# Linear attention and mixture of depths: k and v loaded by halves of partitions, and a reordered end

## Chip, cores and metric

One core of a Trainium2 chip runs the kernel. The metric is the device time of one execution in microseconds (us). The core has five engines that run side by side: TensorE (PE; its weight loads are listed apart as PEld), VectorE (DVE), ScalarE (ACT), GpSimd (POOL) and SyncE (SP). SP and POOL issue DMAs here. The trace comes from one profiled execution, whose own time stands beside its span below.

## The reference

Two blocks follow each other. The first is linear attention over 8 batches of 8 heads, 576 tokens, 64 columns; the second picks 128 of the 576 tokens of each batch and sends them through two dense layers.

```python
q_s = softmax(q, axis=-1)                  # over the 64 columns
k_s = softmax(k, axis=2)                   # over the 576 tokens
kv  = einsum('bhsd,bhse->bhde', k_s, v)
x   = einsum('bhsd,bhde->bhse', q_s, kv)   # then (B, S, H*D) = (8, 576, 512)
scores = x @ w_gate
for b in range(B):
    top = indices of the 128 highest scores[b]
    ye  = relu(x[b, top] @ w1) @ w2        # 512 -> 1024 -> 512
    out[b, top] = x[b, top] + sigmoid(scores[b, top])[:, None] * ye
```

All other rows of out are x. Everything is float32.

## The kernel before

The work is cut into 16 units: a unit is four heads of one batch, so a batch is two units. A head's 576 tokens are 64 runs of 9 tokens. The code writes T = 9, R = 5, N2 = 4, D = 64, P = 128.

**Loads (L118 to L162).** Raw tiles hold k, v and q, three buffers of each (LD = 3). Units 0 and 1 are "flat": a head pair lies on 128 partitions, 9 tokens each, one DMA of 128 partitions with rows of 2304 bytes. From unit 2 on, k and v are "paired": a head lies on all 128 partitions, 5 rows of tokens on each. A run of 9 tokens is split over two neighbouring partitions, 5 tokens on the even one and 4 on the odd one, so that each of k and v takes two DMAs, one to every second partition with 1280-byte pieces and one to the others with 1024-byte pieces (L152). The fifth row of the odd partitions is cleared beforehand (`clear`, L172), and its ones column in v is set to zero there (`fifth`, L311). q of the units in `TWICE` is loaded in a form that VectorE can transpose (L139), 32 partitions at a time; of those in `SPREAD`, the same list here, half of the four DMAs go through POOL's queue. The other q's come in two DMAs, five rows and four rows (L146). From unit 8 on, a load on SP's queue waits until at most DEEP = 4 of these loads are under way (`behind`, L158).

**A unit's arithmetic.** ScalarE takes exp of k (`k_exp`, L289) and of q (`q_exp`, L302 and L298) and copies v beside a column of ones (`v_copy`, L307). `kv_mm` multiplies k by v: for a flat unit in 64x64 quarters of the array (L331), for a paired unit with all 128 partitions as the contraction and two 64-column halves of the array side by side, 5 rows for each of 4 heads (L336). The ones column gives the denominators of k; `kv_out` (L345 to L349) divides and adds a score column. q is transposed on TensorE (`q_t`, L377, L384) or VectorE (`q_blocks`), `x_mm` multiplies it by kv (L405, L409, L414), `x_sums` and `x_scale` (L431 to L442) divide, and `x_store` writes the rows to out from two halves of the partitions, 0 to 63 and 64 to 127 (L452).

**A batch's search.** When a batch's two units are done, `score` sums the scores (L461), `score_row` spreads them over all partitions (TensorE L479, ScalarE L485), `compare` counts how many scores lie before each (L493, five on VectorE), `hits` marks the 128 highest (L510), `find` turns the marks into row numbers (TensorE L520, VectorE L524 to L526), and `fetch` gathers the rows from out with an indirect DMA on POOL (L534). `turn` transposes them (TensorE L571, copy to xT L579).

**The dense layers** are cut into pieces that fill TensorE between the units' steps: eight of `mlp1` (L591, 128x128 products; the ReLU is on ScalarE at L594) and eight of `mlp2` (L601, one 128x512 product each). `finish` scales and adds (L614) and `put` scatters the rows to out with an indirect DMA on POOL (L606).

**Order.** It is written by hand (`manual_schedule`), and each engine's queue runs in that order. The main loop (L793 to L941) has one step s per unit, from LAG = 3 to NU + LAG - 1 = 18. Step s holds the products of unit s, k by v of unit s + 1, exp and copies of later units, one dense layer of batch (s - 3) // 2, and the DMA queue of the step: store of unit s, then loads of k, v and q of unit s + 3. Steps 16 to 18 have no unit left: in 16 the last batch's rows are found and gathered, 17 is its first dense layer, 18 its second. `pieces(n, to)` runs dense pieces at that point of the order. In step 15 three pieces of `mlp1` stand ahead of the last score row (L912), and in step 16 two pieces of `mlp2` ahead of the last search (L879).

```python
        here, follows = s < NU, s + 1 < NU
        ends = s // 2 if here and s % 2 == 1 else None
        chosen = (s - 2) // 2 if s % 2 == 0 and s <= NU else None
```

Of the kernel before, what the change touches and what calls it, by code (L numbers as in the profile page):

```python
# [17 lines left out]
def kernel(  # L18
# [23 lines left out]
    nc = tc.nc  # L42
# [58 lines left out]
    LD = 3  # L101
    FLAT = 0, 1
    TWICE = (9, 11, 13, 14, 15)
    SPREAD = TWICE
    RR = 4 * R
# [12 lines left out]
    def load(u, which, after=None, split=False, flat=False, odd=None):  # L118
        b, qd = units[u]
        for what in which:  # L120
            src = {"q": q, "k": k, "v": v}[what]
            first = src[place(b), 4 * qd].offset
            dmas = []
            if flat:
                t = view(raw[what][u % LD], False)
# [9 lines left out]
            elif what == "q" and u in TWICE:  # L135
                t = raw[what][u % LD].rearrange("p (a n) d -> p a (n d)", a=2)
                for g in range(0, 4, 1 if odd is None else 2):
                    g, queue = (g + 1, nc.gpsimd) if odd else (g, nc.sync)
                    dmas.append(queue.dma_start(out=t[32 * g:32 * g + 32, :, :ROW],  # L139
                                                in_=bass.AP(tensor=src.tensor,  # L140
                                                            offset=first + g // 2 * 2 * SD + g % 2 * D // 2,
                                                            ap=[[2 * T * D, 32], [SD, 2], [1, ROW]])))
            elif what == "q":
                t = view(raw[what][u % LD], False)
                for r0, r1 in ROWS:
                    dmas.append(nc.sync.dma_start(out=t[:, :, r0:r1].rearrange("p i r d -> p i (r d)"),  # L146
                                                  in_=bass.AP(tensor=src.tensor, offset=first + r0 * D,
                                                              ap=[[T * D, P], [2 * SD, 2], [1, (r1 - r0) * D]])))
            else:
                t = view(raw[what][u % LD], True)  # L150
                for n, rows in ((1, N2), (0, R)):
                    dmas.append(nc.sync.dma_start(out=t[n::2, :, :rows].rearrange("p h r d -> p h (r d)"),  # L152
                                                  in_=bass.AP(tensor=src.tensor, offset=first + n * R * D,
                                                              ap=[[T * D, 64], [SD, 4], [1, rows * D]])))
            if after is not None:
# [8 lines left out]
    way = []  # L164
    DEEP = 4
    ROWS = (0, R), (R, T)
# [4 lines left out]

    def clear(u):  # L172
        for what in "kv":
            nc.gpsimd.memset(view(raw[what][u % LD], True)[:, :, N2], 0.0)

# [40 lines left out]
    nc.vector.tensor_scalar(valid, second_half, -1.0, 1.0, op0=OP.mult, op1=OP.add)  # L216
    even_p = const.tile([P, 1], I32, name="even_p")
    nc.gpsimd.iota(even_p, pattern=[[0, 1]], base=1, channel_multiplier=1)
    nc.vector.tensor_single_scalar(even_p, even_p, 1, op=OP.bitwise_and)
    even = const.tile([P, 1], F32, name="even")  # L220
    nc.vector.tensor_copy(out=even, in_=even_p)
    beyond = const.tile([P, 1], F32, name="beyond")
# [27 lines left out]
    nc.gpsimd.iota(whole.rearrange("p (b r) -> p b r", b=B), pattern=[[S, B], [1, R]], base=0, channel_multiplier=T)  # L250
    clear(2)
    dma_k = load(1, "k", flat=True)
# [39 lines left out]
    def q_exp(u, c):  # L292
        if c == 0:
            st["qe", u] = at.tile([P, T, 2, D], F32, tag="qe", name="qe")
        if u in TWICE and u not in FLAT:
            half = raw["q"][u % LD].rearrange("p (a n) (h s) -> p a n h s", a=2, h=2)[:, c, :, 0]
            to = st["qe", u].rearrange("p r i d -> p (r i d)").rearrange("p (a n s) -> p a n s", a=2, n=2 * T)
            nc.scalar.activation(out=to[:, c], in_=half, func=AF.Exp)  # L298
            return
        r0, r1 = ROWS[c]  # L300
        qr = raw["q"][u % LD][:, :2 * T].rearrange("p (i r) d -> p r i d", i=2)
        nc.scalar.activation(out=st["qe", u][:, r0:r1], in_=qr[:, r0:r1], func=AF.Exp)  # L302

    def v_copy(u, engine=nc.scalar):
# [3 lines left out]
        else:  # L308
            engine.tensor_copy(out=out_v, in_=in_v)

    def fifth(u):  # L311
        nc.gpsimd.tensor_copy(out=view(v_ones[u % 2], True)[:, :, N2, D:], in_=even[:, None].to_broadcast([P, 4, 1]))

    def kv_mm(u, crossed=False):
# [16 lines left out]
        for a in range(0 if u in FLAT else 2):  # L333
            for r in range(R):
                for i in range(2):
                    nc.tensor.matmul(out=kv_ps[part(i), a, :D + 1], lhsT=ke[:, 2 * i + a, r], rhs=vo[:, 2 * i + a, r],  # L336
                                     start=(r == 0), stop=(r == N2))
        st["kv", u] = [(slice(0, P), kv_ps[:, :, :D + 1])]
# [54 lines left out]
    def x_mm(u, a, wide=False, tag="x"):  # L393
# [5 lines left out]
        for r in range(R):  # L399
            for i, c in QUARTERS:  # L400
                to = x[part(c), i, r * C:(r + 1) * C]
                if r == N2:
                    if a == 0:
                        rows = by_token[part(i), c, r] if u in TWICE and u not in FLAT else qT[part(i), c, r, 0]
                        last = nc.tensor.matmul(out=to, lhsT=rows, rhs=kw[part(i), c], start=True, stop=True)  # L405
                    continue
                if wide:
# [4 lines left out]
                    continue  # L412
                rows = by_token[part(i), a, R * c + r] if u in TWICE and u not in FLAT else qT[part(i), a, r, c]
                last = nc.tensor.matmul(out=to, lhsT=rows, rhs=kw[part(i), a], start=True, stop=True)  # L414
# [189 lines left out]
    def put(b, n, o):  # L604
# [3 lines left out]
            in_=o[:m], in_offset=None)  # L608

    def finish(b, n):  # L610
        m = slots[n][1]
# [46 lines left out]
    def general():  # L658
        nonlocal FLAT
        FLAT = tuple(range(NU))  # L660
        for n in range(2):
            nc.gpsimd.memset(v_ones[n][:, :, D:], 1.0)
        for b in range(B):
# [79 lines left out]
    x_out(0, 0)  # L743
    clear(3)
    load(3, "kv")
# [10 lines left out]
    x_mm(1, 1)  # L756
    fifth(2)
    x_out(0, 1)
# [11 lines left out]
    q_t(2, 0, wide=True, later=True)  # L770
    clear(4)
    load(4, "kv")
# [13 lines left out]
    k_exp(3)  # L786
    fifth(3)
    v_copy(3)
    LAG = 3
    AFTER = {4: 2}  # L790
    QUEUE = {"odd": "x+0 kv+3 q+3", "even": "x+0 kv+3 q+3", 5: "x+0 kv+3 q+3 x-5 x-4"}
    number = good = None
    for s in range(LAG, NU + LAG):  # L793

# [175 lines left out]
```

## Time and profile before

| what | value |
|---|---|
| median of 3 runs | 208.74 us (208.12 to 213.29) |
| the profiled execution | 209.41 us, span 207.6 us |
| TensorE clock granted | 0.986 |
| PE, PEld, DVE, ACT, POOL busy | 193.1, 146.1, 127.0, 92.1, 40.9 us |
| DMA | 49.43 MB, mean 238 GB/s |
| L591 and L601 (dense layers) on PE | 61.8 and 58.4 us |
| L414 (x) and L336 (k by v) on PE | 22.0 and 19.4 us |
| indirect DMA xr (L534), out (L606) on POOL | 8.5 and 7.2 us |

The page sums busy time over the span, draws the span in 40 slices and follows the chain of work that ended last back from the last instruction. A busy TensorE is not a TensorE at its peak, since matmuls are pipelined and their ends are modelled; a matmul of float32 leaves two records, so that 20 products show as 40. Times in the timeline count from the start of the span. Where an engine's idle time is given, the bracket names what ended it. DMA share is the mean busy share of the core's 16 DMA engines; it may go slightly over 1.

### The profile page before, as it was taken

The numbers are of one execution on the slowest core, as the hardware profiler recorded it, in microseconds if no ns is written. First come the engines' busy times: TensorE is split into PE (matmuls) and PEld (weight loads), VectorE is DVE, ScalarE is ACT, GpSimd is POOL, SyncE is SP. The second block draws the span as 40 slices with busy tenths as digits, with TensorE's granted clock in tenths as the row PEclk, the third lists the DMA queues.
The fourth block names the chain that finished last, engine by engine and source line by source line (L and its number), as shares of the span: only waits on it lengthen the run. The fifth ranks groups of instructions, "written<-read, shape, count | busy, mean of one in ns | idle before, by whom it ended". The sixth has DMA issues, their size and how long they took to land.

```text
span 207.6 us, 6693 instructions
## 1 busy us (share of the span) xinstructions
PE 193.1 (93%) x2801; PEld 146.1 (70%) x2801; DVE 127.0 (61%) x392; ACT 92.1 (44%) x136; POOL 40.9 (20%) x110
## 2 busy tenths in 40 slices
PE   7988899999999999999999999999999999999940
PEld 3576788885698749974897569864896479459510
DVE  5776935897278636957684948766696766432010
ACT  4475877673655814772347516452364012111100
POOL 7302100202020403140222132040402030224010
PEclk9999999999999999999999999999999999999995
DMA  6999999999699999899999899999970434031101
GB/s 219 396 294 344 376 363 371 372 374 351 152 295 285 289 356 381 215 296 261 251 285 280 255 230 262 308 269 233 338 210 18 95 114 114 1 102 54 58 17 41
DMA packets 36599, 49.43 MB, mean 238 GB/s; under 512 B 2513, under 2 KB 30673, under 8 KB 36562
## 3 DMA queue, kind: packets, MB, share of 16 engines
q1 hardware_dynamic: 34336, 41.57, 64.8%
q0 software_dynamic: 2080, 7.06, 11.5%
q8 instruction: 24, 0.39, 0.8%
q10 hardware_dynamic: 146, 0.30, 0.5%
q14 instruction: 13, 0.11, 0.1%
HBM read 37.39 MB, written 11.53 MB: 236 GB/s over the span
## 4 chain that ended last, share of the span: by engine, by line
PE 68%; DMA 21%; DVE 2%; issue 2%; ACT 2%; SPq 1%; POOL 1%; POOLq 0%; ACTq 0%
PE mm L591 22%; PE mm L601 21%; DMA k<-in_k_dram 11%; PE x L414 7%; PE kv L336 6%; DMA xr<-out_dram,idx 6%; DMA out_dram<-xs 4%; PE mm L204 3%; PE x L384 2%; PE mm L571 2%; PE kv L479 1%; PE kv L331 1%; PE x L405 1%; PE x L377 1%; DVE xs L439 1%
## 5 line engine op out<-in xcount | busy, mean ns | idle before, releaser
L591 PE MATMUL mm<-xT,w 128*128 128x128 f32 x512 | 61.8, 278 | 0.5 <-DVE xT L579 0.3
L591 PEld LDWEIGHTS mm<-xT,w 128*128 128x128 f32 x512 | 58.7, 192 | 2.3 <-ACT xT L579 1.0
L601 PE MATMUL mm<-w,hT 128*128 128x512 f32 x128 | 58.4, 599 | 0.0
L601 PEld LDWEIGHTS mm<-w,hT 128*128 128x128 f32 x128 | 23.0, 190 | 23.5 <-issue 23.0
L493 DVE SCALAR_TENSOR_TENSOR junk<-srow,s,not_before 128x576 bf16<-128x576 f32 x40 | 32.7, 818 | 5.2 <-ACT srow L485 4.1
L289 ACT ACTIVATE ke<-k 128x1280 f32<-128x1280 f32 (+1 forms) x16 | 20.2, 1260 | 9.8 <-DMA k<-in_k_dram 9.8
L414 PE MATMUL x<-kv_w,qT 64*64 64x66 f32 x960 | 22.0, 222 | 2.1 <-issue 1.4
L439 DVE TENSOR_TENSOR xs<-x,qrec 128x640 f32<-128x640 f32 (+1 forms) x31 | 23.5, 757 | 0.6 <-issue 0.3
L414 PEld LDWEIGHTS x<-kv_w,qT 64*64 64x64 f32 x960 | 18.7, 133 | 5.2 <-issue 4.3
L307 ACT COPY v_ones<-v 128x1280 f32<-128x1280 f32 x14 | 17.6, 1259 | 6.2 <-DMA v<-in_v_dram 6.2
L336 PEld LDWEIGHTS kv<-v_ones,ke 128*64 128x64 f32 x560 | 17.5, 137 | 3.4 <-issue 2.4
L336 PE MATMUL kv<-v_ones,ke 128*64 128x65 f32 x560 | 19.4, 224 | 0.2 <-ACT srow L485 0.2
L614 DVE SCALAR_TENSOR_TENSOR o<-mm,g,xr 128x512 f32<-128x512 f32 x7 | 5.3, 751 | 23.2 <-PE mm L601 23.2
L534 POOL DMA_INDIRECT xr<-out_dram,idx x8 | 8.5, 1061 | 54.6 <-DVE no L526 15.2
L579 ACT COPY xT<-mm 128x512 f32<-128x512 f32 x7 | 4.1, 585 | 31.5 <-PE mm L571 31.5
L606 POOL DMA_INDIRECT out_dram<-o,idx x7 | 7.2, 1026 | 50.5 <-DVE o L614 43.1
L594 ACT ACTIVATE hT<-mm 128x512 f32<-128x512 f32 x16 | 9.5, 596 | 16.5 <-PE mm L591 16.4
L302 ACT ACTIVATE qe<-q 128x640 f32<-128x640 f32 (+1 forms) x22 | 13.9, 677 | 3.5 <-DMA q<-in_q_dram 3.5
L391 ACT COPY qT<-x 128x640 f32<-128x640 f32 (+1 forms) x18 | 10.8, 648 | 9.0 <-PE x L384 8.2
L345 DVE RECIPROCAL krec<-kv 128x2 f32<-128x2 f32 x16 | 2.7, 170 | 18.8 <-PE kv L336 16.4
L431 DVE RECIPROCAL qrec<-x 128x10 f32<-128x10 f32 (+1 forms) x31 | 6.6, 213 | 9.4 <-PE x L405 7.6
L485 ACT ACTIVATE srow<-kv 128x576 f32<-128x576 f32 x7 | 4.5, 648 | 15.2 <-PE kv L479 15.2
(120 smaller groups left out, 187.3 us busy)
## 6 DMA issues: line engine op xcount, KB each, us to landing
out_dram<-xs SPq DMA_DIRECT2D x16, 320.0 KB
k<-in_k_dram SPq DMA_DIRECT2D x14, 320.0 KB
v<-in_v_dram SPq DMA_DIRECT2D x14, 320.0 KB
w<-in_moe_w_dram SPq DMA_DIRECT2D x8, 512.0 KB
out_dram<-xs SPq DMA_DIRECT2D x16, 256.0 KB
k<-in_k_dram SPq DMA_DIRECT2D x14, 256.0 KB
v<-in_v_dram SPq DMA_DIRECT2D x14, 256.0 KB
q<-in_q_dram SPq DMA_DIRECT2D x9, 320.0 KB
```

The source lines that it names most:

```text
L289: nc.scalar.activation(out=ke, in_=view(raw["k"][u % LD], u not in FLAT), func=AF.Exp)
L302: nc.scalar.activation(out=st["qe", u][:, r0:r1], in_=qr[:, r0:r1], func=AF.Exp)
L307: engine.copy(out=out_v, in_=in_v)
L336: nc.tensor.matmul(out=kv_ps[part(i), a, :D + 1], lhsT=ke[:, 2 * i + a, r], rhs=vo[:, 2 * i + a, r], start=(r == 0), stop=(r == N2))
L391: nc.scalar.copy(out=to, in_=src)
L414: last = nc.tensor.matmul(out=to, lhsT=rows, rhs=kw[part(i), a], start=True, stop=True)
L439: nc.vector.tensor_mul(xs[b][:, :n, qd, :, a].rearrange("p r i d -> p i r d"), x[:, :, :, :D], qrec[:, u, a, :, :n].to_broadcast([P, 2, n, ...
L493: nc.vector.scalar_tensor_tensor(junk, st["srow", b], st["s", b][:, r:r + 1], not_before[:, r], op0=OP.subtract, op1=OP.is_ge, accum_out=s ...
L534: nc.gpsimd.indirect_dma_start(out=xr[:m], out_offset=None, in_=out_rows[:(place(b) + 1) * S], in_offset=bass.IndirectOffsetOnAxis(ap=st[" ...
L591: st["piece"] = nc.tensor.matmul(out=h_ps[:, f % 4 * m:(f % 4 + 1) * m], lhsT=w1[:, d, f * P:(f + 1) * P], rhs=xT[:, d, :m], start=(d == 0 ...
L594: nc.scalar.activation(out=hT[:, f - 3:f + 1, :m], in_=h_ps[:, :4 * m].rearrange("p (f c) -> p f c", f=4), func=AF.Relu)
L601: st["piece"] = nc.tensor.matmul(out=st["y", b, n][:m], lhsT=st["hT", b, n][:, f, :m], rhs=w2[:, f], start=(f == 0), stop=(f == KF - 1))
```

## The change

- k and v of the paired units are loaded in four DMAs of 64 neighbouring partitions instead of two of every second partition. The five-token parts of heads 0 and 2 go to partitions 0 to 63 and the four-token parts to 64 to 127; for heads 1 and 3 the halves are swapped. The pieces keep 1280 and 1024 bytes.
- The fifth row is multiplied in 64x64 quarters, four products over the valid half alone, after four rows of full products. `fifth` and its table go, and the clears move to the start, for all buffers.
- q of the units from 3 on that are not in `TWICE` is loaded flat, in one DMA. q of units 14 and 15 is loaded wholly by SP (`SPREAD` is shorter). DEEP is 6.
- In step 15 one piece in place of three stands ahead of the last score row, and in step 16 one in place of two ahead of the last search (`LASTP`).
- Step 18 goes. The last batch's second layer is computed in two halves of 256 columns, each followed by its own scaling and its own scatter, with row numbers of half rows that `halves` prepares in step 16.

```diff
-    SPREAD = TWICE
+    SPREAD = (9, 11, 13)
...
-            if flat:
+            if flat or (u in FLAT and what != "q") or (what == "q" and u not in TWICE and u > 2):
...
-                for n, rows in ((1, N2), (0, R)):
-                    dmas.append(nc.sync.dma_start(out=t[n::2, :, :rows].rearrange("p h r d -> p h (r d)"),
-                                                  in_=bass.AP(tensor=src.tensor, offset=first + n * R * D,
-                                                              ap=[[T * D, 64], [SD, 4], [1, rows * D]])))
+                for a in range(2):
+                    for n in range(2):
+                        rows = R if n == a else N2
+                        dmas.append(nc.sync.dma_start(out=t[part(n), a::2, :rows].rearrange("p h r d -> p h (r d)"),
+                                                      in_=bass.AP(tensor=src.tensor,
+                                                                  offset=first + a * SD + n * (T - rows) * D,
+                                                                  ap=[[T * D, 64], [2 * SD, 2], [1, rows * D]])))
...
-    DEEP = 4
+    DEEP = 6
...
-    def clear(u):
+    def clear():
         for what in "kv":
-            nc.gpsimd.memset(view(raw[what][u % LD], True)[:, :, N2], 0.0)
+            for n in range(LD):
+                t = view(raw[what][n], True)
+                nc.gpsimd.memset(t[:, :, N2] if n > 1 else t[:, 3:, N2], 0.0)
...
         for a in range(0 if u in FLAT else 2):
-            for r in range(R):
+            for r in range(N2):
                 for i in range(2):
                     nc.tensor.matmul(out=kv_ps[part(i), a, :D + 1], lhsT=ke[:, 2 * i + a, r], rhs=vo[:, 2 * i + a, r],
-                                     start=(r == 0), stop=(r == N2))
+                                     start=(r == 0), stop=False)
+        for i, a in QUARTERS if u not in FLAT else ():
+            nc.tensor.matmul(out=kv_ps[part(i), a, :D + 1], lhsT=ke[part(a), 2 * i + a, N2], rhs=vo[part(a), 2 * i + a, N2],
+                             start=False, stop=True)
...
+    def last_product(b, n):
+        m = slots[n][1]
+        g, xr, idx = st.pop(("g", b, n)), st.pop(("xr", b, n)), st.pop(("idx_h", b, n))
+        half = DM // 2
+        o = sl.tile([P, DM], F32, tag="o", name="o")
+        for h in range(2):
+            c = slice(h * half, (h + 1) * half)
+            y_ps = bank("mm", 2)
+            for f in range(KF):
+                nc.tensor.matmul(out=y_ps[:m, :half], lhsT=st["hT", b, n][:, f, :m], rhs=w2[:, f, c],
+                                 start=(f == 0), stop=(f == KF - 1))
+            nc.vector.scalar_tensor_tensor(o[:m, c], y_ps[:m, :half], g[:m], xr[:m, c], op0=OP.mult, op1=OP.add)
+            nc.gpsimd.indirect_dma_start(
+                out=out_halves[:2 * (place(b) + 1) * S],
+                out_offset=bass.IndirectOffsetOnAxis(ap=idx[:m, h:h + 1], axis=0), in_=o[:m, c], in_offset=None)
...
-    for s in range(LAG, NU + LAG):
+    for s in range(LAG, NU + LAG - 1):
...
-                pieces(1 if here and s not in TWICE else 2)
+                pieces((1 if here and s not in TWICE else 2) if s != NU else LASTP)
                 search()
...
+            if chosen == B - 1:
+                each(halves, chosen)
...
-            pieces(0, to=2 if follows else 3)
+            pieces(0, to=1 if s == NU - 1 else 2 if follows else 3)
...
+    each(last_product, B - 1)
```

More of the change, by code (lines that the diff above doesn't have):

```diff
@@ L101 @@
     LD = 3
-    FLAT = 0, 1
+    FLAT = (0, 1) + ()
     TWICE = (9, 11, 13, 14, 15)
-    SPREAD = TWICE
+    SPREAD = (9, 11, 13)
     RR = 4 * R
@@ L216 @@
     nc.vector.tensor_scalar(valid, second_half, -1.0, 1.0, op0=OP.mult, op1=OP.add)
[L217 to L221, printed above, removed]
     beyond = const.tile([P, 1], F32, name="beyond")
@@ L250 @@
     nc.gpsimd.iota(whole.rearrange("p (b r) -> p b r", b=B), pattern=[[S, B], [1, R]], base=0, channel_multiplier=T)
-    clear(2)
+    clear()
     dma_k = load(1, "k", flat=True)
@@ L294, in q_exp @@
             st["qe", u] = at.tile([P, T, 2, D], F32, tag="qe", name="qe")
-        if u in TWICE and u not in FLAT:
+        if u in TWICE:
             half = raw["q"][u % LD].rearrange("p (a n) (h s) -> p a n h s", a=2, h=2)[:, c, :, 0]
@@ L309, in v_copy @@
             engine.tensor_copy(out=out_v, in_=in_v)
-    def fifth(u):
-        nc.gpsimd.tensor_copy(out=view(v_ones[u % 2], True)[:, :, N2, D:], in_=even[:, None].to_broadcast([P, 4, 1]))
     def kv_mm(u, crossed=False):
@@ L403, in x_mm @@
                     if a == 0:
-                        rows = by_token[part(i), c, r] if u in TWICE and u not in FLAT else qT[part(i), c, r, 0]
+                        rows = by_token[part(i), c, r] if u in TWICE else qT[part(i), c, r, 0]
                         last = nc.tensor.matmul(out=to, lhsT=rows, rhs=kw[part(i), c], start=True, stop=True)
@@ L412, in x_mm @@
                     continue
-                rows = by_token[part(i), a, R * c + r] if u in TWICE and u not in FLAT else qT[part(i), a, r, c]
+                rows = by_token[part(i), a, R * c + r] if u in TWICE else qT[part(i), a, r, c]
                 last = nc.tensor.matmul(out=to, lhsT=rows, rhs=kw[part(i), a], start=True, stop=True)
@@ L608, in put, with halves @@
             in_=o[:m], in_offset=None)
+    out_halves = out.rearrange("b s (h d) -> (b s h) d", h=2)
+    def halves(b, n):
+        m = slots[n][1]
+        idx = sl.tile([P, 2], I32, tag="idx_h", name="idx_h", bufs=n_sl)
+        for h in range(2):
+            nc.vector.tensor_scalar(idx[:m, h:h + 1], st["idx", b, n][:m], 2.0, float(h), op0=OP.mult, op1=OP.add)
+        st["idx_h", b, n] = idx
+    def last_product(b, n):
+        m = slots[n][1]
+        g, xr, idx = st.pop(("g", b, n)), st.pop(("xr", b, n)), st.pop(("idx_h", b, n))
+        half = DM // 2
+        o = sl.tile([P, DM], F32, tag="o", name="o")
+        for h in range(2):
+            c = slice(h * half, (h + 1) * half)
[7 more added lines that the diff above has]
+                out_offset=bass.IndirectOffsetOnAxis(ap=idx[:m, h:h + 1], axis=0), in_=o[:m, c], in_offset=None)
     def finish(b, n):
@@ L658, in general @@
     def general():
[L659 to L662, printed above, removed]
+        nonlocal FLAT, TWICE
+        FLAT, TWICE = tuple(range(NU)), ()
         for b in range(B):
@@ L743 @@
     x_out(0, 0)
-    clear(3)
     load(3, "kv")
@@ L756 @@
     x_mm(1, 1)
-    fifth(2)
     x_out(0, 1)
@@ L770 @@
     q_t(2, 0, wide=True, later=True)
-    clear(4)
     load(4, "kv")
@@ L786 @@
     k_exp(3)
-    fifth(3)
     v_copy(3)
     LAG = 3
+    LASTP = 1
     AFTER = {4: 2}
```

## Prediction

> **What bounds the kernel now.** I read the page's busy shares first, then the chain of waits by time, then the stretches (busy time, DMA share and GB/s of chosen windows), then the timeline of the end. TensorE is the bound for most of the span, and from 41 us on it has almost no gaps:
>
> ```profile
> PE 193.1 (93%) x2801; PEld 146.1 (70%) x2801; DVE 127.0 (61%) x392; ACT 92.1 (44%) x136; POOL 40.9 (20%) x110
> ```
>
> Before 41 us the chain runs through something else: three k loads in a row (start, us, what).
>
> ```profile
> 16.19 7.69 DMA k<-in_k_dram
> ...
> 23.95 7.97 DMA k<-in_k_dram
> ...
> 31.94 7.65 DMA k<-in_k_dram
> ...
> 39.69 1.27 ACT ke L289
> 40.96 0.55 ACT srow L485
> 41.51 0.04 issue
> 41.55 0.45 PE kv L336 x8
> ```
>
> The reader is to see that k of unit 5 lands at 39.6, its exp holds ScalarE's queue, the score row behind it frees the PSUM pair, and only then does TensorE get its next k by v product. So whatever the loads up to k(5) lose or gain goes one to one into the end. What speed they have depends on the partitions they touch (columns: busy us of PE, PEld, DVE, ACT, POOL, then clock, DMA share, GB/s):
>
> ```profile
> core 0: us, PE busy (x) PEld busy (x) DVE busy (x) ACT busy (x) POOL busy (x), PEclk, DMA share, GB/s
> 4.00:9.00 5.00, 4.92 (x80) 2.11 (x79) 3.90 (x17) 2.02 (x3) 2.50 (x6) 1.00 1.04 399
> 12.50:16.00 3.50, 3.13 (x96) 2.83 (x85) 2.71 (x9) 3.02 (x5) 0.00 (x0) 1.00 0.95 292
> 28.00:34.00 6.00, 5.65 (x115) 5.17 (x114) 3.67 (x10) 4.26 (x6) 0.00 (x0) 1.00 1.07 368
> 42.00:52.00 10.00, 10.00 (x187) 7.09 (x183) 8.49 (x29) 5.56 (x10) 1.20 (x1) 1.00 1.04 360
> 140.00:143.00 3.00, 3.00 (x8) 1.33 (x7) 2.23 (x5) 1.60 (x2) 0.00 (x0) 1.00 1.00 203
> 165.00:167.00 2.00, 2.00 (x27) 1.06 (x29) 0.63 (x1) 0.20 (x1) 0.00 (x0) 1.00 0.98 216
> 173.50:175.50 2.00, 2.00 (x20) 2.00 (x19) 1.93 (x5) 0.49 (x1) 0.00 (x0) 1.00 0.98 218
> ```
>
> Row by row: loads of all 128 partitions, 399 GB/s; k(2) and v(2), every second partition, nearly alone, 292; the same kind between weights, 368; a mix with two units' stores in it, 360; q loads of 32 partitions beside a gather, 203; stores alone, each from 64 neighbouring partitions, 216 and 218. The last form is the one that k and v take now, as loads. Last, the end of the program (start, us, engine, and in brackets the idle time before and its releaser):
>
> ```profile
> 183.47 0.63 PE L571 MATMUL mm<-ident,xr 128*128 128x128 f32 x4 [0.32 <-DMA xr<-out_dram,idx]
> 185.11 5.62 PE L591 MATMUL mm<-xT,w 128*128 128x128 f32 x48 [0.15 <-ACT xT L579]
> 186.03 1.00 POOL L606 DMA_INDIRECT out_dram<-o,idx  x1 [3.81 <-DVE o L614]
> 190.75 0.99 POOL L606 DMA_INDIRECT out_dram<-o_gated,idx  x1 [2.43 <-DMA out_dram<-o,idx]
> 199.72 0.75 DVE L614 SCALAR_TENSOR_TENSOR o<-mm,g,xr 128x512 f32<-128x512 f32 x1 [8.53 <-PE mm L601]
> 200.75 0.97 POOL L606 DMA_INDIRECT out_dram<-o,idx  x1 [9.00 <-DVE o L614]
> ```
>
> A put waits for the landing of the put before it: issued 186.03, the next one let go at 190.75, so 4.7 us from issue to landing. The last put has 6.85 us from 200.75 to the span's end.
>
> **The change part by part** (minus is a gain; the sum is for the profiled execution: 209.41 us, span 207.6).
>
> *k by v.* Before, 20 products of 66 columns, two records each: 40 in 1.32 us in the chain, 33 ns a record. After, 16 of these, 32 x 33 ns = 1.06 us, and 4 quarter products, 8 records. The nearest row is L331, quarters of the same tiles: 72 in 1.21 us, 16.8 ns, so 0.13 us. Saved 1.32 - 1.19 = 0.13 us in each of 14 units, 1.8 us, on TensorE's own path from 41 us on. If quarters cost a half's 33 ns, nothing is saved; if the array's change of form costs 0.04 us more, as an "issue" line of the chain does, it is 14 x 0.04 = +0.5. I take -1.6, near L331, with a hundredth or two for the change of form. Range -1.8 to +0.5.
>
> *Loads of k and v up to k(5).* Bytes are unchanged, 0.59 MB (320 + 256 KB) for k or v of a unit, and so are the pieces of 1280 and 1024 bytes. k(2) and v(2): 1.18 MB at 292 GB/s, 4.0 us. k(3), v(3), k(4), v(4), k(5): 2.95 MB at 368, 8.0 us. Together 12.0 us. If all run like stores of 64 neighbouring partitions alone, 4.13 MB / 216 = 19.1, so +7.1 us. If neighbouring partitions do better than every second one, up to 368 becoming 399 and 292 becoming 399, 10.35 us, so -1.7. Which end is nearer? In 42 to 52 us two units' stores of this form run with no loss (360), but they are a third of that stretch's bytes, and each half may pair with something else. Here two thirds of the bytes are such halves, eight in a row. I take half the loss, 266 GB/s: +3.5 us.
>
> The Trainium skill, page "SBUF — State Buffer", section "Door 1: The DMA port swizzle", speaks against this change: speed goes by how many of 16 ports the partitions reach, partitions 0 to 63 reach eight, and 64 partitions measured 196 GB/s where 128 had 328. Its section "Can I just issue two DMAs to hit both halves?" gives a second transfer on the other half only 6% more. The trace's stores alone agree (216, 218), its mixed stretch (360) does not. By that rule, 196 x 1.06 = 208 GB/s as an estimate, this term would be 4.13 / 208 - 12.0 = +7.8 us, and the sum 215.6.
>
> *SP's issues.* k and v take 8 issues a unit where they took 4. Four of 256 pieces cost 0.60 us at least (L152); one of 128 pieces 0.40 (L128). Eight at 0.40 and one flat q at 0.47 make 3.7 us for 1.77 MB, 480 GB/s: SP stays ahead of the DMA. If each still costs 0.60, 5.3 us, 335 GB/s, and three and a half units lose 3.5 x 0.5 = +1.6. I take 0. Eight loads can be under way, as before, so 1.2 MB in place of 2.4; at 368 GB/s that is 3.2 us of work, still a full queue.
>
> *q in one flat load* (units 3 to 8, 10, 12). q(3) and q(4) lie ahead of k(5): 1.18 MB, at 368 then at 399 GB/s, 3.2 against 2.95: -0.25. Range -0.25 to 0.
>
> *Steady part, 45 to 165 us.* Slower k and v also land later here, by about 1 us a load at 266 GB/s. v(13) lands at 130.93, its copy ends at 132.2 and the product comes at 134.37: 2.1 us of cover. v(14): copy ends 142.45, product 143.58: 1.1. v(15): 155.9 to 157.67: 1.8. On the other side, q(14) and q(15) leave POOL's queue, which costs SP four issues of 0.52 us after v and frees the gather at 136.49, which took 8.73 us where a quiet one (179.94) took 3.40; TensorE's wait for it is 0.30 us at 145.27. DEEP 6 of half-size loads lets 0.9 MB run where 4 let 1.2: no cost while DMA has other work, and it shortens what stands ahead of the next store. I take +0.5. Range -0.3 to +3.0 (1 us at each of those three v loads).
>
> *Pool's clears* move to the start (six memsets of at most 0.30 us before 5 us), the fifth-row copies (0.19 to 0.32 us) and two tiny VectorE operations go. POOL is idle for 10 us after 9 us: nothing. Were that cover gone, the first load of k(2), issued at 9.70, would wait at most the memsets' 1.2 us.
>
> *Rows and search sooner.* Scores are ready at 170.04 (L461 at 169.81); with one piece ahead in place of three TensorE reaches the row at 168.97 + 0.98 = 169.95 and waits 0.1 us. The compares start when VectorE has scaled, 171.78, in place of 173.25, so hits end near 176.9 and the find, one piece (0.86 us) sooner, near 177.8, waits for nothing. The gather then has six pieces of cover (5.2 us) for its 4.7 us from find to landing, and the 0.32 us at 183.47 go. The 0.15 us at 185.11 stay: transposes 0.63 and one piece 0.86 against 1.64 us until xT is copied. -0.32 + 0.12 = -0.2. Range -0.47 to +0.15.
>
> *Last product halved.* Let T be its start, 192.81. Before: last put issued at T + 7.94. After: the first half's 16 records take half of 6.88, its VectorE step about 0.45 (half of 0.75 and a fixed part), the hand-over 0.27: first put at T + 4.2. Both write the same rows of out, so in the built program the second put waits for the first one's landing: T + 4.2 + 4.7 = T + 8.9, although its data is ready at T + 7.6. That is 0.95 us later than before; half the bytes in each put give back up to 0.3 twice. I take +0.6; range -0.3 (no wait, shorter VectorE step) to +0.95. The two index operations (about 0.15 us each) are on an idle VectorE.
>
> **Sum:** -1.6 + 3.5 + 0 - 0.25 + 0.5 + 0 - 0.2 + 0.6 = +2.55 us. From 209.41 the profiled execution comes to 212.0; it stood 0.67 above the median of 208.74, so the median comes to 211.3.
>
> **The rivals.**
> *Halves cost nothing.* For it: 360 GB/s in 42 to 52 us with stores of halves inside. Against it: 216 whenever they are alone. Without the load terms of 3.5 and 0.5: 207.3.
> *Slower, halves run at the speed of stores alone, through and through* (216 GB/s). Place: the loads up to k(5), +7.1 in place of 3.5; then each batch, where k, v 2.36 MB / 216 = 10.9, q 4.4, stores 5.5, gather and put 1.4 make 22.2 us of DMA against a period of 22.25 us (score rows at 60.27 and 82.52), so late v loads cost about +2 in place of 0.5. 211.3 + 3.6 + 1.5 = 216.4. It decides (over 2%) from about 241 GB/s down: 4.13 / 241 = 17.1, +5.1 us. [...]
> *Faster:* neighbouring partitions are better than every second one (-1.7) and the steady part frees the gather (-0.3): 211.3 - 5.2 - 0.8 = 205.3, and past 2% only if the end gains 0.3 as well (204.4).
>
> **How the numbers follow.** Forecast, half the loss: 0.50; no loss: 0.22; full loss: 0.24; faster: 0.04. A measurement of this kernel can tell about 2% from no change, 204.6 to 212.9. Over 212.9 lie the full loss and about 0.12 of the forecast's 0.50 (its loads near 240 GB/s): 0.36. Below 204.6: the best part of the two gaining cases, 0.06. Between: 0.58. The range leaves out the faster case and the upper end of the full loss: 206.3 to 216.8; the forecast's own is 208.8 to 213.5.
>
> **What would show it.** In the chain, the k loads before 41 us longer than 23.3 us together; in 12.5 to 16 us GB/s near 216 and in 28 to 34 below 368 (near 368 makes the second step wrong and the time 207). L336 as quarters near 17 ns a record and each unit's products 1.19 us. Idle time of TensorE before L571 at the last search gone, 0.1 us before the last score row. Second last put started only when the first has landed, over 4 us after it. TensorE waiting for v copies between 120 and 160 us would be the full loss.

## The result, and the profile after

The changed kernel takes 222.85 us (median of 6 runs, 218.99 to 225.64) against 208.81 us for the kernel before on the same chip; the ratio is 1.054, interval 1.044 to 1.063. It is slower, by about 11 us, and lies outside the forecast's range. The profiled execution took 223.27 us with a span of 221.5 us; it was one of the four longer runs of the six, which the ratio leaves out (the other two took 218.99 and 220.88 us), so its times serve to show where the time goes rather than how much it is.

The busy times are close to those before (TensorE 197.0 us against 193.1); the span has grown by waiting:

```profile
PE 197.0 (89%) x2817; PEld 151.8 (69%) x2817; DVE 127.4 (58%) x393; ACT 92.3 (42%) x136; POOL 37.2 (17%) x104
```

The stretches of the changed kernel, with the same columns as in the prediction (busy us of PE, PEld, DVE, ACT, POOL, then clock, DMA share, GB/s):

```profile
4.00:9.00 5.00, 4.88 (x82) 2.32 (x81) 4.20 (x18) 2.42 (x3) 0.79 (x4) 1.00 1.05 402
12.50:16.00 3.50, 3.19 (x89) 2.78 (x85) 2.58 (x10) 2.46 (x5) 0.00 (x0) 1.00 0.87 211
28.00:34.00 6.00, 4.35 (x99) 3.97 (x97) 2.64 (x8) 2.25 (x3) 0.00 (x0) 1.00 1.06 326
42.00:52.00 10.00, 5.12 (x63) 4.58 (x63) 4.18 (x11) 4.22 (x6) 0.75 (x4) 0.83 1.09 309
```

The flat loads still run at 402 GB/s. k(2) and v(2) have fallen from 292 to 211, the mixed stretch from 368 to 326, and from 42 to 52 us TensorE is busy for half of the time where it had no gap. Where the DMA share is 1.06 at 326 GB/s the DMA engines are occupied and slow; where it is 0.87 at 211 they are also left without work. What leaves them without work is seen on SP's queue, first in the kernel before, then in the changed one (count, then shortest, median and longest issue in ns):

```profile
L152 SPq DMA_DIRECT2D k<-in_k_dram x28: 607/1014/2030, 9.7 to 143.3; - x28
L152 SPq DMA_DIRECT2D v<-in_v_dram x28: 601/604/1271, 11.3 to 145.2; - x28
```

```profile
L154 SPq DMA_DIRECT2D k<-in_k_dram x56: 595/612/1553, 9.1 to 162.6; - x56
L154 SPq DMA_DIRECT2D v<-in_v_dram x56: 595/605/2371, 12.0 to 165.3; - x56
```

The shortest issues take 0.60 us whether they carry two heads or four, and so does the median for v; for k the median was 1.01 us before and is 0.61 now. There are twice as many, and 0.59 MB of a unit's k or v in four DMAs is 147 KB each, so SP cannot hand out more than 147 KB in 0.60 us, 245 GB/s, while it issues k and v. From 9.15 to 16.63 us the chain of the changed kernel is SP's issues, one behind the other. After that SP is held by something else as well (the chain's lines; start, us, what):

```profile
16.16 0.47 SPq L192
16.68 8.07 DMA w<-in_moe_w_dram
24.77 0.59 SPq L154
...
36.41 6.13 DMA q<-in_q_dram
42.56 5.22 DMA v<-in_v_dram
```

Loads of v are issued at 24.77 and 42.56 us, each within 0.02 us of the landing of the load that was issued eight places earlier, at 16.68 and 36.41. So SP waits here until fewer than eight loads are under way, and with half-size loads of k and v among them eight hold fewer bytes than before. No run changes that number, so its share of the loss is not known.

The late loads then reach TensorE twice (start, us, engine, and in brackets the idle time before and its releaser):

```profile
45.96 1.27 ACT L289 ACTIVATE ke<-k 128x1280 f32<-128x1280 f32 x1 [6.37 <-DMA k<-in_k_dram]
47.13 0.63 ACT L485 ACTIVATE srow<-kv 128x576 f32<-128x576 f32 x1
...
112.19 1.26 ACT L307 COPY v_ones<-v 128x1280 f32<-128x1280 f32 x1 [6.04 <-DMA v<-in_v_dram]
```

```profile
34.35 0.98 PE L384 MATMUL x<-ident,qe 64*128 64x64 f32 x18 [2.00 <-ACT qe L302]
...
47.82 1.96 PE L333 MATMUL kv<-v_ones,ke 128*64 128x65 f32 x32 [4.88 <-ACT srow L485]
...
113.50 2.00 PE L333 MATMUL kv<-v_ones,ke 128*64 128x65 f32 x32 [3.24 <-ACT v_ones L307]
```

The exp of k(5) starts at 45.96 in place of 39.69; the score row sits behind it, and TensorE waits 4.88 us for that. At 113.50 it waits for v(10), which ScalarE could copy only at 112.19. In both places the 32 products that follow take 1.96 and 2.00 us where they take 1.08 elsewhere (the chain's lines below). The reason is the clock that was granted after each wait (same columns as above):

```profile
47.60:51.00 3.40, 3.18 (x44) 2.94 (x45) 2.31 (x7) 2.46 (x4) 0.00 (x0) 0.54 1.07 379
...
113.40:116.80 3.40, 3.30 (x44) 2.84 (x44) 0.74 (x3) 0.05 (x1) 0.00 (x0) 0.50 0.78 251
116.80:120.20 3.40, 3.40 (x81) 3.18 (x81) 1.76 (x9) 1.74 (x3) 0.19 (x1) 0.59 0.84 224
```

At 0.54 for 3.4 us, and at 0.50 and 0.59 for twice 3.4 us, the clock takes another 1.6 and 3.1 us of TensorE's work, as an estimate from these shares.

How far behind the kernel before the score rows (TensorE's L479 and what stands for it) of batches 2 to 7, counted from 0, start, in us from the timelines. The head gives their starts in the kernel before:

| kernel | 60.27 | 82.52 | 104.50 | 126.62 | 149.84 | 171.75 |
|---|---|---|---|---|---|---|
| changed | +9.4 | +9.7 | +16.7 | +16.8 | +15.6 | +13.2 |
| before, with two DMAs on halves | +13.0 | +12.9 | +12.5 | +11.9 | +10.9 | +9.2 |
| before, with four DMAs on every second partition | +7.4 | +8.6 | +14.8 | +14.2 | +16.9 | +15.2 |
| halves in units 2 to 5 only | +12.0 | +12.1 | +11.9 | +11.8 | +10.9 | +9.7 |
| halves from unit 6 on only | -0.1 | +0.5 | +2.7 | +2.8 | +1.8 | -0.6 |

The changed kernel loses 9.4 us up to the row of batch 2 and 7.0 us near 113 us, and gains back some 3.6 by the row of batch 7. The other rows belong to experiments told below. The loss near 113 us is in the kernel with twice the DMAs (+8.6 to +14.8) and not in the one with halves (+12.9 to +12.5).

### The profile page after: what moved, and what is told of

It reads as the page before. It is cut to its first block, busy times and chain, and to the rows that moved or that the text cites. A ratio compares the mean times of both kernels' runs of the same rounds, so it can differ in the third digit from the quotient of the medians.

```text
span 221.5 us, 6793 instructions
## 1 busy us (share of the span) xinstructions
PE 197.0 (89%) x2817; PEld 151.8 (69%) x2817; DVE 127.4 (58%) x393; ACT 92.3 (42%) x136; POOL 37.2 (17%) x104
## 3 DMA queue, kind: packets, MB, share of 16 engines
q1 hardware_dynamic: 33376, 42.72, 67.1%
## 4 chain that ended last, share of the span: by engine, by line
PE 68%; DMA 19%; SPq 5%; ACT 2%; issue 2%; POOL 0%; POOLq 0%; DVE 0%; ACTq 0%
PE mm L591 24%; PE mm L601 20%; PE x L414 7%; DMA v<-in_v_dram 6%; PE kv L333 6%; DMA q<-in_q_dram 6%; DMA w<-in_moe_w_dram 4%; SPq L154 3%; PE mm L628 3%; DMA k<-in_k_dram 3%; PE x L384 2%; PE mm L571 2%; PE kv L479 2%; PE kv L336 2%; ACT qT L391 1%
## 5 line engine op out<-in xcount | busy, mean ns | idle before, releaser
L591 PE MATMUL mm<-xT,w 128*128 128x128 f32 x512 | 62.5, 280 | 0.3 <-DVE xT L579 0.3
L591 PEld LDWEIGHTS mm<-xT,w 128*128 128x128 f32 x512 | 59.5, 194 | 2.1 <-ACT xT L579 0.7
L601 PE MATMUL mm<-w,hT 128*128 128x512 f32 x112 | 51.3, 600 | 0.0
L601 PEld LDWEIGHTS mm<-w,hT 128*128 128x128 f32 x112 | 20.1, 190 | 20.1 <-issue 19.6
L289 ACT ACTIVATE ke<-k 128x1280 f32<-128x1280 f32 (+1 forms) x16 | 20.1, 1258 | 16.9 <-DMA k<-in_k_dram 12.1
L333 PE MATMUL kv<-v_ones,ke 128*64 128x65 f32 x448 | 17.8, 238 | 8.3 <-ACT srow L485 4.9
L414 PE MATMUL x<-kv_w,qT 64*64 64x66 f32 x960 | 22.8, 228 | 2.5 <-issue 2.3
L307 ACT COPY v_ones<-v 128x1280 f32<-128x1280 f32 x14 | 17.6, 1256 | 16.7 <-DMA v<-in_v_dram 16.0
L333 PEld LDWEIGHTS kv<-v_ones,ke 128*64 128x64 f32 x448 | 15.8, 149 | 11.8 <-ACT srow L485 5.1
L639 DVE SCALAR_TENSOR_TENSOR o<-mm,g,xr 128x512 f32<-128x512 f32 x6 | 4.5, 750 | 14.5 <-PE mm L601 14.5
L606 POOL DMA_INDIRECT out_dram<-o,idx x6 | 6.2, 1029 | 39.6 <-DVE o L639 39.6
L463 POOL TENSOR_TENSOR s<-s_all,valid_r 128x5 f32<-128x5 f32 x8 | 1.6, 194 | 62.3 <-DVE s_all L461 62.3
```

The lines of the kernel that those rows point to most:

```text
L289: nc.scalar.activation(out=ke, in_=view(raw["k"][u % LD], u not in FLAT), func=AF.Exp)
L307: engine.copy(out=out_v, in_=in_v)
L591: st["piece"] = nc.tensor.matmul(out=h_ps[:, f % 4 * m:(f % 4 + 1) * m], lhsT=w1[:, d, f * P:(f + 1) * P], rhs=xT[:, d, :m], start=(d == 0 ...
L601: st["piece"] = nc.tensor.matmul(out=st["y", b, n][:m], lhsT=st["hT", b, n][:, f, :m], rhs=w2[:, f], start=(f == 0), stop=(f == KF - 1))
```

## The experiments

Two theories stood at the start. Ports: 64 neighbouring partitions take data more slowly than every second partition. Issues: SP needs the same time for half the data. A third was added after the profile: the clock's halving makes the waits costlier than the late data alone would. "Ratio" is to the kernel before on the same chip, with its interval.

| label | what it is | ratio |
|---|---|---|
| b_halves2 | before, two DMAs on neighbouring halves | 1.064 (1.057 to 1.071) |
| b_split4 | before, four DMAs on every second partition | 1.075 (1.064 to 1.086) |
| b_halves4 | before, four DMAs, each half twice running | 1.089 (1.078 to 1.101) |
| b_halves4alt | before, four DMAs, halves in turn | 1.075 (1.070 to 1.081) |
| b_rest | before with all of the change but k and v | 0.993 (0.989 to 0.996) |
| b_qflat | before, q flat and SPREAD shorter | 0.994 (0.990 to 0.997) |
| b_nosplit | b_qflat with rows and search sooner | 0.994 (0.991 to 0.997) |
| b_search | before, rows and search sooner | 1.000 (0.997 to 1.003) |
| b_tail | before, last product halved | 1.000 (0.997 to 1.003) |
| a_two | changed, two DMAs of five rows | 1.072 (1.062 to 1.082) |
| a_warm | changed, with idle products in the waits | 1.058 (1.052 to 1.064) |
| a_early | changed, halves in units 2 to 5 only | 1.045 (1.040 to 1.050) |
| a_late | changed, halves from unit 6 on only | 0.999 (0.995 to 1.003) |
| a_full | changed, fifth rows not in quarters | none, see below |
| a_act | changed, half of the early issues on ScalarE | 1.133 (1.127 to 1.139) |

**Each cause alone.** b_halves2 changes only where the two DMAs go, b_split4 only how many there are; b_halves4 and b_halves4alt do both. The edits, shortened to what differs:

```diff
 b_halves2 (here and in the last two the ones column of the fifth row goes by halves, too)
-  out=t[n::2, :, :rows]
+  out=t[part(n), :, :rows]
 b_split4 (and DEEP = 6)
-  out=t[n::2, :, :rows]            ap=[[T * D, 64], [SD, 4], [1, rows * D]]
+  for a in range(2):
+      out=t[n::2, a::2, :rows]     ap=[[T * D, 64], [2 * SD, 2], [1, rows * D]]
 b_halves4 (and DEEP = 6), b_halves4alt with the loops over a and n exchanged and 0 to 63 first
+  for a in range(2):
+      out=t[part(n), a::2, :rows]  ap=[[T * D, 64], [2 * SD, 2], [1, rows * D]]
```

> The kernel before, with k and v in four DMAs a tensor, each still of every second partition (two heads each), and DEEP 6. Theory P (ports: a load into 64 neighbouring partitions moves near 216 GB/s, and the number of issues does not matter): as before, 208 to 210 us, and k(2), v(2) in 12.5 to 16 us near 290 GB/s. Theory S (SP: each issue costs about 0.64 us whatever its size, so k and v of a unit, 1.18 MB in eight issues, can't move faster than 230 GB/s, and partitions do not matter): nearly all of the loss, 216 to 221 us, and those two loads near 230 GB/s.

> The kernel before, with its two DMAs for each of k and v, but into 64 neighbouring partitions in place of every second one (and the ones column of the fifth rows masked to match). Theory P: most of the loss, 215 to 220 us, k(2) and v(2) near 216 GB/s, k of unit 5 landing near 45 us. Theory S: as before, 208 to 210 us, k of unit 5 landing near 39.6 us.

> The kernel before with both: four DMAs a tensor, into 64 neighbouring partitions, heads not swapped, five full rows, DEEP 6. Theory P: as two halves, 215 to 220 us. Theory S: as four of every second partition, 216 to 221 us. If both count, more than either alone, 219 to 224 us.

> The kernel before with four DMAs a tensor into 64 neighbouring partitions, as in the earlier run of four, but with the halves in turn (0 to 63, 64 to 127, 0 to 63, 64 to 127), as the changed kernel has them, in place of the same half twice. Theory P with engines that drift: halves in turn can overlap, so less than 1.089 of before, near 1.06 to 1.07. If the order does not matter: 1.085 to 1.09 again, and the changed kernel's better 1.054 must come from elsewhere.

The stretch of k(2) and v(2), first with twice the DMAs, then with halves:

```profile
12.50:16.00 3.50, 3.12 (x87) 2.78 (x80) 2.58 (x10) 2.37 (x4) 0.00 (x0) 1.00 0.66 177
28.00:34.00 6.00, 5.79 (x122) 5.27 (x121) 3.03 (x9) 4.03 (x5) 0.00 (x0) 1.00 1.05 363
```

```profile
12.50:16.00 3.50, 3.11 (x67) 2.55 (x57) 2.65 (x10) 3.17 (x5) 0.00 (x0) 1.00 1.11 231
28.00:34.00 6.00, 5.24 (x104) 4.86 (x104) 3.63 (x10) 3.02 (x3) 0.00 (x0) 1.00 1.09 283
```

The two causes have different marks. With twice the DMAs the engines are busy for two thirds of the time (0.66) and keep 363 GB/s where weights are queued as well. With halves they are always busy (1.11) and slow in both stretches. The exp of k(5), at 39.69 us before, starts at 44.33 with twice the DMAs and at 50.29 with halves. Each alone costs as much as the whole change or more, and both together little beyond that: they limit the same loads. b_split4 also has DEEP = 6 and, like the changed kernel, fewer bytes in eight loads under way; these were not tested apart from the count of issues. Taking the halves in turn looks better than the same half twice running (1.075 and 1.089), but the intervals overlap. With the 0.993 of the rest, b_halves4alt would come to 1.068, where the changed kernel has 1.054; the difference may be due to the swapped heads or the quarters, and no run separates these.

**The loads by themselves.** A kernel with nothing but loads of 64 partitions, nine stretches of 2.62 MB each; nothing of the reference is computed. It ran once.

```diff
+    phase([every], 4, [nc.sync])          # every second partition, 0.33 MB a DMA
+    phase([low], 4, [nc.sync])            # 0 to 63
+    phase([mid], 4, [nc.sync])            # 32 to 95
+    phase([low, high], 4, [nc.sync])      # 0 to 63 and 64 to 127 in turn
+    phase([every], 2, [nc.sync])          # and with half the size:
+    phase([mid], 2, [nc.sync])
+    phase([low], 2, [nc.sync])
+    phase([every], 2, [nc.sync, nc.scalar])
+    phase([low], 2, [nc.sync, nc.scalar])
```

> Loads by themselves: nothing of the reference is computed, out gets one block of zeros. Nine stretches one after the other, each 2.62 MB in pieces of 1280 bytes. With eight DMAs of 0.33 MB on SP's queue: (1) into every second partition, (2) into 0 to 63, (3) into 32 to 95, (4) into 0 to 63 and 64 to 127 in turn. With sixteen of half the size: (5) every second, (6) 32 to 95, (7) 0 to 63, then (8) every second and (9) 0 to 63 with the issues shared between SP and ScalarE. Theory P (ports): 2, 4, 7 and 9 near 215 GB/s; 1 and 3 near 290 or more, although 3 is 64 neighbouring partitions too. If neighbours as such are slow, 3 is as slow as 2. Theory S (issues): 5 and 6 near 230 GB/s at half-busy DMA engines, and 8 back at the speed of 1; 9 stays at 215.

One window inside each of the nine stretches, in that order (busy us of DVE and POOL, clock, DMA share, GB/s):

```profile
6.00:15.00 9.00, 5.25 (x5) 0.00 (x0) 1.00 0.85 243
19.00:30.00 11.00, 0.00 (x0) 0.00 (x0) 1.00 1.09 205
33.00:41.00 8.00, 0.00 (x0) 0.00 (x0) 1.00 0.94 318
45.00:55.00 10.00, 0.00 (x0) 0.00 (x0) 1.00 1.06 221
59.00:68.00 9.00, 0.00 (x0) 0.00 (x0) 1.00 0.85 242
72.00:81.00 9.00, 0.00 (x0) 0.00 (x0) 1.00 0.88 247
85.00:97.00 12.00, 0.00 (x0) 0.00 (x0) 1.00 1.02 196
101.00:108.00 7.00, 0.00 (x0) 0.00 (x0) 1.00 0.90 287
113.00:123.00 10.00, 0.00 (x0) 0.00 (x0) 1.00 1.10 205
```

The first row is not the speed of its loads. Each of them waits until VectorE has cleared its tile, and the clears follow each other every 1.34 us, which for 0.33 MB is 245 GB/s (SP's wait in us, times and longest; then two of the clears):

```profile
SPq L45 <- DVE raw L22: 7.0, 8, 2.1
6.97 1.12 DVE L22 MEMSET raw<- 128x1280 f32 x1 [0.21 <-issue]
8.31 1.12 DVE L22 MEMSET raw<- 128x1280 f32 x1 [0.22 <-issue]
```

The other rows can be compared. 64 neighbouring partitions are not slow as such: 32 to 95 run at 318, 0 to 63 at 205. Halving the size brings 318 down to 247 and leaves 0 to 63 at 196. The 247, and the 242 of the fifth row, are SP's issues: it hands out the sixteen loads of such a stretch in 10.3 and 10.4 us, near 250 GB/s. A second issuing queue lifts every second partition from 242 to 287 and 0 to 63 only from 196 to 205. So both limits are real, near 245 GB/s by SP's issues at 164 KB a load and near 205 by the half of the partitions, and the lower one decides. The Trainium skill, page "SBUF — State Buffer", section "Door 1: The DMA port swizzle", gives a formula by which 0 to 63 reach eight ports and 32 to 95 all sixteen; these two rows, 205 and 318, agree with it.

**Early or late.** The changed kernel with the old loads and full fifth rows for part of the units.

```diff
+    OLD = tuple(range(2, 6))     # a_late; a_early: range(6, 16)
+    for n, rows in ((1, N2), (0, R)) if u in OLD else ():
+        dmas.append(nc.sync.dma_start(out=t[n::2, :, :rows].rearrange("p h r d -> p h (r d)"),
...
-    for a in range(2):
+    for a in range(0 if u in OLD else 2):
```

> The changed kernel with halves and quarters for units 2 to 5 only; from unit 6 on k and v are loaded, and their fifth rows multiplied, as before. If the loss lies in the loads up to k(5), as the forecast had it (+3.5 us early, +0.5 later), it stays: the profile's +6.3 us less the 1.5 that the rest gains, ratio about 1.023. If the steady part loses as much by itself, this kernel gives back more than half of the 5.4%; if the steady part has slack that makes up for a late start, the ratio falls below 1.01.

> The reverse: units 2 to 5 as before, halves and quarters from unit 6 on. By the forecast 0.5 us of loss and 1.5 of gain: ratio 0.995. By the profile of the changed kernel, in which TensorE stood still again near 113 us and the clock fell to half (about 7 us): 1.025 to 1.035, with a wait of TensorE for a v copy of over 2 us between 100 and 160 us.

a_early keeps 1.045 of 1.054: most of the loss belongs to the loads of units 2 to 5. a_late, 0.999, stands 0.5 to 0.7% above the kernels with only the rest of the change (0.993 and 0.994), about 1.3 us for halves in ten units; the intervals are 0.4% wide to each side, and its twelve runs reach from 207.06 to 214.50 us, so this is a rough size. a_early has no second stall: by the table above it stays 12 us behind from 60 us on. The one at 113 us thus needs both, late loads at the start and the four DMAs after. By the same table b_split4 has it, and b_halves2, whose loads are late and slow as well but in two DMAs, has not. Whether it is the issues, DEEP or the bytes under way was not tested. In a_early TensorE's wait came from the same place:

```profile
50.96 2.00 PE L350 MATMUL kv<-v_ones,ke 128*64 128x65 f32 x32 [3.11 <-ACT srow L502]
```

Its exp of k(5) came at 49.10, 3 us later than in the changed kernel with the same early loads. Part of it may be the difference between executions: a_warm, with the changed kernel's loads, had 48.50. So a_early's ratio may put the early share somewhat too high.

**Issues moved to ScalarE.**

```diff
-    dmas.append(nc.sync.dma_start(
+    dmas.append((nc.scalar if a and u < 6 else nc.sync).dma_start(
```

> The changed kernel with the loads of heads 1 and 3 of k and v of units 2 to 5 issued by ScalarE in place of SP. If SP's 0.60 us an issue holds the early loads, 12.5 to 16 us rises from 211 GB/s towards 270, k(5) lands some 3 us sooner and the ratio falls to about 1.04. If it is the 64 neighbouring partitions, as in the loads measured alone (201 GB/s from two queues, 191 from one), the stretch stays at 200 to 230 and the ratio at 1.05 or, by ScalarE's issues, above.

(In the windows shown above, the loads alone into 0 to 63 have 205 GB/s from two queues and 196 from one.) 12.5 to 16 us rose to 275 GB/s, as the issues would have it, but ScalarE then stood at its own issues: each took 0.60 us, but the two of a tensor, with the wait between them, held it for 2.35 us (k) and 5.76 us (v). TensorE waited 10.22 us, until 28.47 us, for an exp of q. The kernel became slower still (1.133). The run doesn't tell the two causes apart; it shows that ScalarE had no room for the issues at this place.

**Two DMAs that still fill halves.** Five rows go into both halves, so one token of each run is loaded twice (11% more bytes); it is used once, and the quarters take the row that is then left on one half. The edit is shortened.

```diff
+    for n in range(2):
+        out=t[part(n)]   offset=first + n * N2 * D   ap=[[T * D, 64], [SD, 4], [1, R * D]]
```

> The changed kernel with k and v in two DMAs a tensor again, into partitions 0 to 63 and 64 to 127, five rows into both (the middle token twice, so 11% more bytes), quarters kept on the row that stands once; no clears. Takes away theory S's part and keeps theory P's. If ports alone made the loss: as the changed kernel or 1 to 2% slower for the bytes (1.05 to 1.07 of before). If issues made half of it: 1.03 to 1.05.

The first stretch rose from 211 to 254 GB/s at a share of 1.11, the second fell to 301, and TensorE waited 3.94 and 6.14 us: no gain. The loss stays without the extra issues, here with 11% more bytes.

**The clock.** Idle products ahead of k by v of units 4 and 10.

```diff
+            fill(14)
             kv_mm(4)
...
+            if s == 9:
+                fill(10)
```

> The changed kernel with idle products of ones put where TensorE waited longest in its profile: 14 ahead of unit 4's k by v (4.9 us of waiting), 10 ahead of unit 10's (3.2 us), each about 0.25 us. Theory C (a wait of 3 us or more also costs clock: the granted clock fell to half for 3.4 and 6.8 us after them): the clock stays up and 2 to 5 us come back, 1.03 to 1.045 of before. Otherwise: no gain, 1.05 to 1.06.

The mean clock was 0.979 (0.970 in the profile of the changed kernel, up to 0.976 in its other runs), and the time stayed at 1.058. The waits moved (1.68 us at 22.2, 2.12 at 44.5, 2.86 at 67.1), and half clock followed the first and the last of them for 3.4 us each, 6.8 us in place of 10.2. So this edit won nothing, but it did not keep the clock up either, and what half clock alone costs stays open. That a faster TensorE only reaches the next late load sooner would fit, and is not shown.

**The rest of the change, and its parts.** Their diffs are those of the front: b_rest has all but k and v; b_tail has `last_product`, b_search `LASTP` and `to=1`, b_qflat the flat q and SPREAD, b_nosplit the last two together.

> The kernel before with all of the change but the k and v loads, the quarters and DEEP: q flat, SPREAD shorter, last rows and search sooner, last product halved. By the prediction's steps -0.25 (q), -0.2 (search), +0.6 (tail), and the gather freed: 208 to 210 us under both theories. Much above 211 us would say that neither P nor S is the whole cause.

> The kernel before with the last product halved and nothing else. As the prediction has it, the second scatter waits for the first one's landing: +0.6 us, ratio 1.003, and in the timeline the second put starts 4.7 us after the first. By the profile of the changed kernel, in which the second put started as soon as VectorE had its half: 0.4 us gained, ratio 0.998, second put 3.4 us after the first, the span's end 14.4 us after the last product's start.

> The kernel before with the last score row and the last search one or two pieces sooner and nothing else. Prediction: -0.2 us, at most -0.47, ratio 0.999; TensorE's idle 0.32 us before the last transposes at 183.5 us gone. Rival, that the later search is not what made that wait but the gather itself: the wait stays, ratio 1.000 or above.

> The kernel before with q flat from unit 3 on and q of units 14 and 15 wholly on SP, nothing else. Prediction: -0.25 us from the loads up to k(5), and TensorE's wait of 0.30 us near 145 us gone: -0.5 us, ratio 0.997 to 0.998. If the three other parts together gained 1.5 us because SP has fewer issues early on, most of it is here: ratio 0.995, and the exp of k(5) starts near 39.1 us in place of 39.7.

> The kernel before with rows and search sooner and q flat (SPREAD shorter), the last product whole. All three parts together gave 0.9926 on another chip. If the halved last product gains 0.4 us, this one stands at 0.9945; if it loses 0.6 us as predicted, this one stands at 0.990 and is the best version.

b_rest is the best version run: 203.4 us against 205.3 on its chip, faster by 0.4 to 1.1%. The gain is that of b_qflat, which alone has 0.994 (q flat and SPREAD together); the other two parts cannot be told from nothing.

**Quarters.**

```diff
-    for r in range(N2):                 # and four quarter products
+    for r in range(R):                  # fifth row over both halves, cleared where no token is
```

> The changed kernel with its loads, but the fifth rows as full products over both halves with a cleared invalid half, as before. If quarters save what the forecast said (1.6 us), this one is slower than the changed kernel by 0.008, ratio 1.062. By the chain of the changed kernel (1.36 us a unit against 1.32) it is the same or faster by 0.003: 1.051 to 1.054.

Undecided: its six runs took 215.22 to 222.49 us (median 221.73, before 208.82), too wide for a difference of under 1%. What the quarters cost is read from the chain of the changed kernel instead:

```profile
52.54 1.08 PE kv L333 x32
53.62 0.28 PE kv L336 x8
```

1.36 us together in this unit, against 1.32 for the full products before.

## Why the prediction was wrong

The place was right, and so was the kind of loss. Most of it arises up to k(5), through exp, score row and PSUM pair, as the first part said, and a_early shows it. What failed were sizes, above all that of SP's issues, put at 0, and that of the loads up to k(5), and one thing that was left out.

- **SP's issues.** The step took 0.40 us for a half-size issue, from a flat load, and set SP's rate for k, v and q together (480, at worst 335 GB/s). It is 0.60 us, and k and v leave SP in a row of eight, without q: 245 GB/s at most. b_split4, with the count of DMAs and DEEP alone changed, costs 7.5%. The step also took eight loads under way for a full queue, and the chain has SP waiting for the eighth load back, where the chain before ran through three loads of k. The nearest row was L152, with the same partitions in one DMA, and the step had it as its bad bound; the bound was too low since q was averaged in.
- **Loads of k and v up to k(5).** +3.5 us was forecast as half of the loss, 266 GB/s. The exp of k(5) came 6.3 us later, close to the bound of 7.1, and the stretch ran at 211 GB/s, near the 216 of stores alone; the nearness is in part luck, since the issues hold this stretch too, and with halves alone (b_halves2) the exp came 10.6 us later. The mixed stretch at 360 GB/s, which spoke for half, held halves and other DMAs side by side; here eight halves are issued in a row. The step's "two thirds of the bytes" is also wrong: it counts k, v and q, but six loads of weights of 0.52 MB lie between k(2) and k(5), which makes it 4.13 of 9.05 MB. The rule of the page that the prediction set aside was the better guide: the loads by themselves gave 205.
- **What followed the late load.** It had no term. After TensorE's wait of 4.88 us the clock was at half for 3.4 us, and k(6)'s exp slipped from 49.90 to 58.24; by the score row of batch 2 the 6.3 us had become 9.4. How much of that is the clock's was not tested.
- **Steady part.** +0.5 us, at most 3. By itself it is about 1.3 us (a_late), inside that range. In the changed kernel it is 7.0 us near 113 us: v(10) made TensorE wait 3.24 us, and by the estimate above half clock took 3.1 us more. By the table of score rows it goes with the four DMAs after a late start; the step had no more than 1 us a load.
- **k by v.** -1.6 us was forecast from the 16.8 ns of quarters in a long row of quarters. Eight records after full products took 35 ns each: 0.04 us lost in that unit, which in 14 units is the upper bound of that step.
- **q in one flat load.** -0.25 us was forecast, from the loads up to k(5); together with the shorter SPREAD it gave 0.3 to 1.0%, 0.5 to 2.0 us. The place was wrong: in b_qflat's profile the exp of k(5) starts at 39.90, no sooner than 39.69, and its score rows, counted as above, stand at +0.2 or +0.3 for batches 2 to 5 and at -0.6 and -0.4 for 6 and 7, so there the gain comes late. What brings it was not tested.
- **Rows and search sooner.** -0.2 us was forecast; measured 0 within 0.3%, which cannot tell the two apart. TensorE's wait ahead of the last transposes is gone, as forecast.
- **Last product halved.** +0.6 us was forecast because the second put would wait for the first one's landing. It did not:

```profile
211.35 0.97 POOL L631 DMA_INDIRECT out_dram<-o,idx_h  x1 [4.99 <-DVE o L630]
214.80 0.96 POOL L631 DMA_INDIRECT out_dram<-o,idx_h  x1 [2.48 <-DVE o L630]
```

The second put starts 3.45 us after the first, as soon as VectorE has its half, and the span ends 14.4 us after the product's start where it had been 14.8. Alone the part is worth nothing that could be measured (1.000).

Of the rivals, "slower" had the mechanism, halves at the speed of stores alone, and a price of 216.4 us. It lacked the issues, which hold the same loads from a second side, and the fall of the clock.

## What to carry to other kernels

Before a load is cut into more DMAs, multiply the issue time of the nearest row by the new count for the tensors that are issued in a row, without the others that may come between; if that is below the speed the loads had, the cut is likely to be a loss. Whether loads of part of the partitions are slow is read from a stretch that holds nothing else, not from a mixed one. In these traces a late load that left TensorE idle for 2.5 us or more was always followed by half clock, so the products after it were slower too; what that costs in the end was not separated. A stretch that is to show the speed of loads must also be free of anything else that paces them, as the clears did in the first stretch here.

## What the runs showed of the hardware

- An issue on SP to 64 partitions took 0.60 us at the shortest with 128 pieces as with 256, and a load of 128 partitions 0.37 to 0.47 at the shortest.
- Loads to partitions 0 to 63 ran at 205 GB/s, to 32 to 95 at 318, to every second partition at 287 from two queues (242 from one, held by the issues).
- TensorE's clock fell to half after waits of 4.88 us (for 3.4 us) and 3.24 us (for 6.8 us), and it stayed at 1.00 after the wait of 2.00 us at 34.35. Over all profiles half clock came with every wait of 2.5 us or more (nineteen), and with five of the twelve between 1.5 and 2.3 us: after 1.68 us (a_warm) and 1.98 (b_halves2), but not after 2.12 (a_warm) or 2.25 (b_split4). The Trainium skill, page "TensorE: Matmul & The Clock Gate", section "Part 1: The HAM clock gate (the "warmup" mystery)", speaks of windows of about 3.4 us, running freely, and of half clock after an idle one. The lengths at half clock fit, 3.4 and twice 3.4; a whole idle window was not needed, as the waits of 1.68 to 3.24 us show.
- The stretch from 12.5 to 16 us varies by itself: with k and v loaded as before it had 275 to 349 GB/s over seven kernels, so that only the larger differences there count.
